# Other slots for eight early weight tiles, and the maxima of v two heads at a time, in a talking-heads attention with a gated MLP behind it

## The chip, the cores and the metric

One core of a Trainium2 chip runs the whole program. The metric is the device time of one execution in microseconds. Smaller is better. The median of three runs stands for a kernel, and one further execution was recorded by the hardware profiler.

## What is computed

```python
# attention: batch 4, heads 12, sequence 448, head_dim 64
scores = einsum('bhij,hg->bgij', q @ k^T / 8, w_pre)      # mixed over heads before the softmax
attn   = exp(scores - max) / (sum + 1e-9)                 # over the keys
attn   = einsum('bhij,hg->bgij', attn, w_post)            # mixed over heads behind it
x      = attn @ v, as 1792 tokens x 768
# gated MLP, w_gate and w_val 768 x 1536, w_out 1536 x 768; the MLP's weights come as 8-byte floats
out    = (1 / (1 + exp(-(x @ w_gate))) * (x @ w_val)) @ w_out
```

## The kernel before, in words

**Stages.** The program is one instruction stream per engine, written out by hand in program order. First comes the attention (`_attention`), up to about 344 us of the span. Behind it comes the MLP (`_Moe`), whose tasks a planner in the kernel has put in order. The MLP's first operands are prepared while the attention's last slots run.

**Blocks, units, slots.** A batch's 448 query rows are cut into four blocks of 120, 120, 120 and 88 rows, sixteen blocks in all. A block is cut into sets of ten rows, and two sets are a unit: six units in a block of 120, five in the last block of a batch, whose fifth unit holds one set. That makes 23 units a batch and 92 in all. The attention's main loop (L396) runs over slots s. The blocks begin at slots 0, 6, 12, 18, then 23, 29, 35, 41, then 46, 52, 58, 64, then 69, 75, 81, 87. A batch's last block is slots 18 to 22, 41 to 45, 64 to 68 and 87 to 91.

**What one slot issues.** GpSimd scales the sums of unit s+1 (`norm`, L228, result ss), VectorE takes their reciprocal (L229), and GpSimd scales the exponentials to fp16 (`scale`, L235, result ph, two instructions). TensorE mixes the heads of unit s+2 (`premix`, L211). VectorE takes row maxima (`rowmax`, L216, result nm). TensorE computes the scores of a pair of heads of a later block (`scores`, L157), and ScalarE and VectorE copy one half each out of PSUM (`keep`, L163). ScalarE takes the exponentials of unit s+2 (`expo`, L223, result e, with an accumulator read for the sums). VectorE computes the rest of the fp16 split (`p_lo`, L241, result pl, which reads e and ph from SBUF). Then come the small VectorE jobs of the plan (`v_max`, L175; `v_bound`), TensorE's second mix of unit s (`postmix`, L253), ScalarE's copy of it (`mix`, L261), and last the "tail": the product with v for an earlier block (`av`, L280) and the early weight steps. A second pair of scores in the same slot follows the tail.

**Which scores and products a slot has.** The scores of a block are issued five slots ahead of the block before it, so those of a batch's last block (88 rows, padded to 90) lie in slots 7 to 12, 30 to 35, 53 to 58 and 76 to 81. They take four matmuls where others take eight. Slots 13, 36 and 59 hold two pairs of scores. The products with v of a last block (88 columns) lie in slots 23 to 28, 46 to 51 and 69 to 74, and slots 18, 41, 64 and 87 hold two products.

**Early weight tiles.** Eight of the MLP's weight tiles (k = 0 to 7) are loaded and turned from 8-byte floats into fp32 within the attention. `EARLY_AT[k]` is a tile's base slot, and `early(k, step)` is issued at base + 1, 2, 3, 4 (four loads on SP's queue, L1028), + 6 and 7 (the first GpSimd step, in two halves, L1067, from int8 into the buffer `half`), + 8 (a GpSimd cast within `half`, L1075), + 9 and 10 (the last GpSimd step, in two halves, L1067), + 10 and 11 (two halves of `convert` on VectorE, L1083), + 11 and 12 (two ScalarE passes `sum_of`, L989, which take a sum into an accumulator and write their unwanted output into the first half of `half`), and + 13 (`keep_w`, a DMA that GpSimd issues, L1087). There is one buffer `half` for all tiles, and three raw buffers, used in turn. Tiles 3 and 7 also carry the steps of a bound (`early_bound`), from base + 13 on.

The tail of a slot is issued in the order in which the plan was filled, so a step of tile k stands ahead of one of tile k+1:

```python
    for k in range(moe.EARLY):
        for step, slot in enumerate((1, 2, 3, 4, 6, 7, 8, 9, 10, 10, 11, 11, 12, 13)):
            at(EARLY_AT[k] + slot, moe.early, k, step)
```

**Maxima of v.** `v_max(b, h)` reduces head h of v (256 elements a partition) to one number, 48 instructions in all. `v_bound(b, step)` makes a bound of them for each pair of batches; its step 0 is three small VectorE instructions.

Of the kernel before, what the change touches and what calls it, by code (L numbers as in the profile page):

```python
# [25 lines left out]
QUAD = 4  # L26
# [15 lines left out]
def _attention(ctx, tc, ins, B, H, S, D, xs, raws, make_moe):  # L42

    nc = tc.nc
# [47 lines left out]
    vm = const.tile([128, B * H], F32, name="vm")  # L92
# [73 lines left out]
    vt = {}  # L166
# [5 lines left out]


    def v_max(b, h):
        nc.vector.tensor_reduce(vm[:, H * b + h:H * b + h + 1], vt[b, h // QUAD][:, h % QUAD].rearrange("p j d -> p (j d)"),  # L175
                                axis=AX.X, op=ALU.max, apply_absolute_value=True)

    def v_bound(b, step):
# [116 lines left out]

    LEAD = 5
    SOFT = 2
    EARLY_AT = (5, 12, 19, 27, 34, 42, 49, 57)
    BOUND = (0, 6, 10, 11, 12, 13, 14)
    plan = {}  # L300

    def at(slot, fn, *args):
        plan.setdefault(slot, []).append((fn, args))

    def spread(i, n, s0, s1):
        return s0 + i * (s1 - s0) // n

    taken = {EARLY_AT[k] + slot for k in range(moe.EARLY) for slot in (10, 11)}
    for b in range(B):
        f = first[PB * b]  # L310
        for u in range(NQ):
            at(f + 2 + 2 * u, v_load, b, u)
        s = f + 5
        for h in range(H):
            s = max(s + 1, f + 6 + 2 * (h // QUAD))
            while s in taken:
                s += 1
            at(s, v_max, b, h)
        if b % 2:
            at(s + 1, v_bound, b, 0)  # L320
        if b == 1:
            for step, slot in enumerate(BOUND[1:]):
                at(s + 1 + slot, v_bound, b, step + 1)
        for c in range(NP if b else 0):
            at(spread(c, NP, first[PB * (b - 1)] + 6, first[PB * b - 1] - LEAD - 2), k_load, b, c)
# [15 lines left out]
# [3 lines that stand above are left out]
        if k % 4 == 3:  # L344
            for step, slot in enumerate((13, 14, 17, 19, 20, 21, 22, 22)):
                at(EARLY_AT[k] + slot, moe.early_bound, ("w", k // 4), step)

# [852 lines left out]
@with_exitstack  # L1200
def kernel(ctx, tc, B, H, S, D, ins, out):
    nc = tc.nc
    top = ctx.enter_context(tc.tile_pool(name="top", bufs=1))
    dram = ctx.enter_context(tc.tile_pool(name="dram", bufs=1, space=DRAM))
    xs = dram.tile([B, H * D // 128, 128, S], F32, name="xs")
    with tc.manual_schedule():
        raws = top.tile([128, 13 * H * D // 2], F32, name="raws")
        with ExitStack() as c2:
            moe = _attention(c2, tc, ins, B, H, S, D, xs, raws,
                             lambda NG: _Moe(tc, xs, ins, out, raws, NG, top))  # L1210
        moe.run()
# [72 lines left out]
```

## Time and profile before

| | us |
|---|---|
| median of 3 runs | 788.52 (788.35 to 790.19) |
| the profiled execution | 788.24 |
| its span, first to last instruction | 786.5 |
| TensorE busy | 760.4 (97%) |
| VectorE busy | 649.4 (83%) |
| ScalarE busy | 548.3 (70%) |
| GpSimd busy | 293.7 (37%) |

The granted TensorE clock is 0.998 of full speed over the span. Matmuls are pipelined and their ends are modelled, so a busy TensorE is not TensorE at its peak. What a slot takes is read from the start of one unit's premix (L211) to the start of the next unit's: slot s begins with the premix of unit s+2. The chain of waits, followed back from the last instruction of a stretch, names what released each piece.

### The profile page before, as it was taken

To read this page: it belongs to the slowest core of one execution; us is meant where nothing else is said; L and a number is where in the kernel's file an instruction comes from. 1 tells how busy PE (TensorE), PEld (TensorE's weight loads), DVE (VectorE), ACT (ScalarE), POOL (GpSimd) and SP (SyncE) were. 2 spreads that over 40 slices of the span, in tenths; PEclk is the share of its full clock that TensorE was granted. 3 is DMA by queue.
4 is the path that set the end of the run, shared out by engine and by line. 5 is a ranking of instruction groups with operands and counts; after the bars stand their busy time and mean duration, and the time that the engine had idled before them with its cause. 6 is when DMAs were issued, how large, how long until landed. Compare 5 with 4: busy or idle time off the path is not lost.

```text
span 786.5 us, 23288 instructions
## 1 busy us (share of the span) xinstructions
PE 760.4 (97%) x9530; PEld 417.6 (53%) x9530; DVE 649.4 (83%) x1116; ACT 548.3 (70%) x1058; POOL 293.7 (37%) x462
## 2 busy tenths in 40 slices
PE   7899999999999999888999999999999999999998
PEld 2455655565556555564555455555555555555554
DVE  4999999999989999999996989589876999997111
ACT  3887889788978888796875876577756784563000
POOL 1447776876786544410222222224222221010000
PEclk9999999999999999999999999999999999999999
DMA  5786568756875575839406284663567788995001
GB/s 183 232 255 223 192 231 260 252 193 227 284 261 186 183 226 186 250 105 321 143 27 224 92 301 152 251 222 141 198 205 263 277 313 312 383 346 206 36 36 70
DMA packets 80714, 166.13 MB, mean 211 GB/s; under 512 B 20448, under 2 KB 57664, under 8 KB 80608
## 3 DMA queue, kind: packets, MB, share of 16 engines
q1 hardware_dynamic: 72304, 132.88, 51.0%
q0 software_dynamic: 7728, 31.27, 10.3%
q8 instruction: 74, 1.21, 0.7%
q10 hardware_dynamic: 576, 0.51, 0.2%
q14 instruction: 32, 0.26, 0.1%
HBM read 87.77 MB, written 38.15 MB: 160 GB/s over the span
## 4 chain that ended last, share of the span: by engine, by line
PE 77%; ACT 9%; DVE 7%; DMA 3%; POOL 2%; issue 2%; SPq 0%; ACTq 0%; DVEq 0%; POOLq 0%
PE bank L1138 31%; PE bank L1149 18%; PE av L280 8%; PE pm L211 7%; PE qk L157 7%; PE mx L253 6%; ACT e L223 3%; ACT mix L261 2%; DVE nm L216 2%; DVE m L1122 2%; DMA k<-in_kp_dram 1%; ACT st L163 1%; ACT m L1117 1%; DVE m L1131 1%; DVE pl L241 1%
## 5 line engine op out<-in xcount | busy, mean ns | idle before, releaser
L1138 PEld LDWEIGHTS <-m 128*128 128x128 f16 x1512 | 147.5, 98 | 143.6 <-DVE m L1122 4.1
L1138 PE MATMUL bank<-m,m 128*128 128x448 f16 x1116 | 214.7, 352 | 4.6 <-DVE m L1122 3.2
L223 ACT ACTIVATE e<-pm,nm 128x448 f32<-128x448 f32 x180 | 115.2, 640 | 50.1 <-DVE nm L216 42.1
L235 POOL TENSOR_SCALAR ph<-e,ss 128x448 f16<-128x448 f32 x180 | 113.2, 641 | 55.3 <-DVE ss L229 31.3
L241 DVE SCALAR_TENSOR_TENSOR pl<-e,ss,ph 128x448 f16<-128x448 f32 x180 | 123.6, 725 | 1.2 <-POOL ph L235 1.2
L1149 PEld LDWEIGHTS <-m 128*128 128x128 f16 x756 | 74.0, 98 | 69.0
L216 DVE TENSOR_REDUCE nm<-pm 128x1 f32<-128x448 f32 x180 | 103.0, 613 | 7.2 <-PE pm L211 5.4
L253 PEld LDWEIGHTS <-ph 64*128 64x128 f16 x2880 | 67.6, 93 | 68.0 <-issue 34.5
L261 ACT ACTIVATE mix<-mx 128x960 f32<-128x960 f32 (+1 forms) x92 | 103.0, 1119 | 0.0
L157 PE MATMUL qk<-k,q 64*64 64x448 f32 (+2 forms) x640 | 94.9, 545 | 4.4 <-ACT st L163 2.8
L211 PE MATMUL pm<-T,w 64*64 64x448 f32 (+1 forms) x720 | 95.3, 560 | 1.3 <-ACT e L223 0.7
L280 PE MATMUL av<-mix,v 128*64 128x120 f32 (+1 forms) x1504 | 92.6, 267 | 1.4 <-ACT xt L290 1.4
L1149 PE MATMUL bank<-m,m 128*128 128x448 f16 x468 | 92.9, 352 | 0.0
L1075 POOL CAST raws<-raws 128x768 f16<-128x768 bf16 x36 | 40.6, 1127 | 117.4 <-ACT raws L1069 117.4
L253 PE MATMUL mx<-w2hi,ph 64*128 64x60 f16 x1440 | 70.9, 188 | 9.3 <-ACT mix L261 8.9
L1138 PE MATMUL bank<-m 128*128 128x448 f16 x396 | 77.9, 353 | 0.0
L280 PEld LDWEIGHTS av<-mix,v 128*64 128x64 f32 x1504 | 73.5, 137 | 6.2 <-ACT xt L290 1.7
L253 PE MATMUL mx<-w2hi,pl 64*128 64x60 f16 x1440 | 70.4, 187 | 0.2 <-DVE pl L241 0.2
L253 PE MATMUL mx<-w2lo,ph 64*128 64x60 f16 x1440 | 70.5, 187 | 0.0
L1165 DVE TENSOR_TENSOR m<-bank,m 128x448 f32<-128x448 f32 x72 | 44.4, 619 | 22.1 <-PE bank L1138 13.9
L253 PEld LDWEIGHTS <-pl 64*128 64x128 f16 x1440 | 61.7, 93 | 0.3 <-DVE pl L241 0.3
L228 POOL TENSOR_SCALAR ss<-ss 128x2 f32<-128x2 f32 (+1 forms) x92 | 30.2, 328 | 81.4 <-ACT e L223 79.0
(124 smaller groups left out, 1079.3 us busy)
## 6 DMA issues: line engine op xcount, KB each, us to landing
T<-st SPq DMA_DIRECT2D x176, 210.0 KB
m<-w SPq DMA_DIRECT2D x60, 384.0 KB
raws<-in_w_dram SPq DMA_DIRECT2D x28, 767.6 KB
hs<-m POOLq DMA_DIRECT2D x48, 224.0 KB, 3.2
m<-hs SPq DMA_DIRECT2D x15, 672.0 KB
w<-m POOLq DMA_DIRECT2D x21, 384.0 KB, 4.7
w<-raws POOLq DMA_DIRECT2D x20, 384.0 KB, 4.5
v<-in_vb_dram SPq DMA_DIRECT2D x12, 512.0 KB
```

What stands on the lines that cost most here:

```text
L157: nc.tensor.matmul(sc[e][s0:s1, :S], lhsT=q[rows, c, s0:s1], rhs=k[rows, :], start=True, stop=True)
L211: nc.tensor.matmul(pm[bank][64 * x:64 * x + 64, :S], lhsT=w1[rows], rhs=T[rows, x], start=True, stop=True)
L216: nc.vector.tensor_reduce(nm[:, i:i + 1], pm[bank][:, :S], axis=AX.X, op=ALU.max, negate=True)
L223: nc.scalar.activation(out=e_t[u][:, i], in_=pm[units[u][2][i]][:, :S], func=AF.Exp, bias=nm_t[u][:, i:i + 1], scale=1.0, accum_out=ss_t[u ...
L235: nc.gpsimd.tensor_scalar(ph[:, i], e_t[u][:, i], ss_t[u][:, i:i + 1], 1.0, op0=ALU.mult, op1=ALU.mult)
L241: nc.vector.scalar_tensor_tensor(pl[:, i], e_t[u][:, i], ss_t[u][:, i:i + 1], p_t[u][0][:, i], op0=ALU.mult, op1=ALU.subtract)
L253: nc.tensor.matmul(mx[:, x, i, jb * HK:(jb + 1) * HK], lhsT=p[rows, i, JB[jb]:JB[jb] + 128], rhs=w[rows], start=(k == 0), stop=(k == 2))
L261: nc.scalar.activation(out=out.rearrange("p g (y r) -> p y g r", r=HALF), in_=mx_t.pop(u), func=AF.Copy, scale=1.0 / (P_UP * W_UP))
L280: nc.tensor.matmul(av_t[bi][64 * i:64 * i + 64, c % 4, :n], lhsT=vt[b, u][:, h + i, jb, :], rhs=mixes[bi % 2][:, jb, 2 * c + i, :n], start ...
L1138: self.nc.tensor.matmul(self.f32(bank), lhsT=w[a][:, k], rhs=x[b][:, k], start=self.START[i] and k == r == 0, stop=k == self.KH - 1 and r ...
L1149: self.nc.tensor.matmul(self.f32(bank), lhsT=w[a][:, k], rhs=b[bb], start=self.START[i] and j == k == r == 0, stop=j == OUT_TILES - 1 and ...
L1165: self.nc.vector.tensor_tensor(self.f32(out), self.f32(bank), self.f32(snap), op=ALU.add)
```

## The change

`EARLY_AT` gets other base slots, `v_max` takes two heads in one instruction (a 2 x 256 input, two results) every second slot, and `v_bound` of batch 1 keeps its slot by an explicit line.

```diff
     def v_max(b, h):
-        nc.vector.tensor_reduce(vm[:, H * b + h:H * b + h + 1], vt[b, h // QUAD][:, h % QUAD].rearrange("p j d -> p (j d)"),
+        at = h % QUAD
+        nc.vector.tensor_reduce(vm[:, H * b + h:H * b + h + 2], vt[b, h // QUAD][:, at:at + 2].rearrange("p h j d -> p h (j d)"),
                                 axis=AX.X, op=ALU.max, apply_absolute_value=True)
...
-    EARLY_AT = (5, 12, 19, 27, 34, 42, 49, 57)
+    EARLY_AT = (-1, 6, 13, 19, 30, 37, 53, 60)
...
-        s = f + 5
-        for h in range(H):
-            s = max(s + 1, f + 6 + 2 * (h // QUAD))
+        s = f + 4
+        for h in range(0, H, 2):
+            s = max(s + 2, f + 6 + 2 * (h // QUAD))
             while s in taken:
                 s += 1
             at(s, v_max, b, h)
+        if b == 1:
+            s = f + 23
         if b % 2:
             at(s + 1, v_bound, b, 0)
```

Worked out from the code, the slots of each tile's five GpSimd steps, and of its two ScalarE passes:

| tile | steps before | passes before | steps after | passes after |
|---|---|---|---|---|
| 0 | 11-15 | 16, 17 | 5-9 | 10, 11 |
| 1 | 18-22 | 23, 24 | 12-16 | 17, 18 |
| 2 | 25-29 | 30, 31 | 19-23 | 24, 25 |
| 3 | 33-37 | 38, 39 | 25-29 | 30, 31 |
| 4 | 40-44 | 45, 46 | 36-40 | 41, 42 |
| 5 | 48-52 | 53, 54 | 43-47 | 48, 49 |
| 6 | 55-59 | 60, 61 | 59-63 | 64, 65 |
| 7 | 63-67 | 68, 69 | 66-70 | 71, 72 |

The pairs of maxima stand in slots 6, 8, 11, 13, 15, 18; 31, 33, 35, 37, 39, 42; 52, 54, 56, 58, 60, 62; and 75, 77, 79, 81, 83, 85. `v_bound` of batch 1 begins in slot 47 in both kernels, that of batch 3 in slot 86 instead of 87.

## Rows read from the trace of the kernel before

**Rows 1.** Busy time by stretch: window, its length, then each engine, clock, DMA.

```profile
400.00:420.00 20.00, 20.00 (x108) 10.32 (x106) 18.79 (x24) 12.05 (x20) 3.67 (x7) 1.00 0.39 131
```

**Rows 2.** Chain of waits, slots 80 and 81 (90-wide scores): start, us, what.

```profile
303.03 0.91 PE pm L211 x8
...
306.49 0.91 PE pm L211 x8
```

**Rows 3.** Chain of waits, slots 70 to 75 (products 88 columns wide).

```profile
269.78 0.91 PE pm L211 x8
...
285.77 0.91 PE pm L211 x8
```

**Rows 4.** Chain of waits, starts of slots 16, 18 and 23.

```profile
77.47 0.91 PE pm L211 x8
78.39 0.75 PE qk L157 x8
...
84.28 0.91 PE pm L211 x8
...
101.77 0.91 PE pm L211 x8
```

**Rows 5.** Chain of waits, early slots: GpSimd's small step of two units.

```profile
33.03 0.33 POOL ss L228
...
36.05 0.33 POOL ss L228
```

**Rows 6.** VectorE's maxima of v, 27 to 330 us: xcount | busy us, mean ns | idle.

```profile
L175 DVE TENSOR_REDUCE vm<-v 128x1 f32<-128x256 f32 x48 | 19.6, 408 | 0.0
```

**Rows 7.** Timeline of GpSimd, slots 56 to 58: start, us, instruction, [idle before].

```profile
219.15 0.19 POOL L228 TENSOR_SCALAR ss<-ss 128x2 f32<-128x2 f32 x1
...
220.94 2.43 POOL L1067 TENSOR_SCALAR raws<-raws 128x384 int16<-128x384 int8 x1
223.46 0.19 POOL L228 TENSOR_SCALAR ss<-ss 128x2 f32<-128x2 f32 x1
...
227.39 0.19 POOL L228 TENSOR_SCALAR ss<-ss 128x2 f32<-128x2 f32 x1
...
231.69 0.19 POOL L228 TENSOR_SCALAR ss<-ss 128x2 f32<-128x2 f32 x1
```

**Rows 8.** Timeline of VectorE beside it, slot 56.

```profile
221.04 1.27 DVE L241 SCALAR_TENSOR_TENSOR pl<-e,ss,ph 128x448 f16<-128x448 f32 x2
```

**Rows 9.** Timeline of TensorE: starts of slots 34, 38, 48, 53, 56 and 61.

```profile
139.55 0.61 PE L211 MATMUL pm<-T,w 64*64 64x448 f32 x4
...
155.73 0.61 PE L211 MATMUL pm<-T,w 64*64 64x448 f32 x4
...
189.85 0.61 PE L211 MATMUL pm<-T,w 64*64 64x448 f32 x4
...
207.05 0.61 PE L211 MATMUL pm<-T,w 64*64 64x448 f32 x4
...
217.44 0.61 PE L211 MATMUL pm<-T,w 64*64 64x448 f32 x4
...
238.82 0.61 PE L211 MATMUL pm<-T,w 64*64 64x448 f32 x4
```

**Rows 10.** Timelines of ScalarE (slots 24, 25) and GpSimd (slots 25, 26).

```profile
109.88 0.52 ACT L989 ACTIVATE raws<-raws 128x384 f16<-128x384 f32 x1
...
112.02 1.18 ACT L261 ACTIVATE mix<-mx 128x960 f32<-128x960 f32 x1
...
111.66 1.55 POOL L1067 TENSOR_SCALAR raws<-raws 128x384 int16<-128x384 int8 x1
...
115.09 1.20 POOL L1067 TENSOR_SCALAR raws<-raws 128x384 int16<-128x384 int8 x1
```

**Rows 11.** Timeline of VectorE, slots 86 to 88.

```profile
326.51 1.15 DVE L1122 SCALAR_TENSOR_TENSOR m<-m,one_w 128x384 f16<-128x384 f32 x2 [0.91 <-ACT m L1117]
...
330.60 0.21 DVE L999 STREAM_TRANSPOSE junk<-one_x 128x32 f32<-128x32 f32 x1
```

## The prediction, made before the changed kernel was run

> **What bounds the kernel now.** I read the page's shares first, then the chain of waits stretch by stretch, then the timelines of GpSimd and VectorE where the chain left TensorE. Behind the attention TensorE is busy without a gap [rows 1], so what the attention ends earlier or later, the kernel does too, nearly one for one. The change lies wholly within the attention, so the question is what bounds a slot there.
>
> The page shows VectorE at 83% and nearly full in the attention, and one would take it for the bound. The chain says otherwise. In most slots it runs from premix to scores to second mix to product and back to premix, with TensorE alone. With 90-wide scores a slot takes 306.49 - 303.03 = 3.46 us [rows 2]; with 120-wide scores and 120-wide products (84.28 - 77.47) / 2 = 3.40 us [rows 4]; with 88-wide products (285.77 - 269.78) / 5 = 3.20 us [rows 3]. I call these the floors. A second pair of scores adds about 0.75 us [rows 4], so slots 13, 36 and 59 have a floor of about 4.15. Only in slots 1 to 6, which have no product yet, is a latency loop longer than TensorE's work: from GpSimd's sums through VectorE's reciprocal and maxima, ScalarE's two exponentials and back to GpSimd, 36.05 - 33.03 = 3.02 us [rows 5]. The same loop turns in every slot, so the others have a slack of 3.46 - 3.02 = 0.44, 0.38 and 0.18 us. What delays the loop by less costs nothing.
>
> What the early steps cost today is then the time of a stretch less its floors. Slots 34 to 37: 155.73 - 139.55 = 16.18, floors 2 x 3.46 + 4.15 + 3.40 = 14.47, so 1.7 us. Slots 56 to 60: 238.82 - 217.44 = 21.38, floors 3 x 3.46 + 4.15 + 3.40 = 17.93, so 3.4 us. Slots 48 to 52: 207.05 - 189.85 = 17.20, floors 4 x 3.20 + 3.40 = 16.20, so 1.0 us [rows 9]. But slots 18 to 22, which hold all five steps of tile 1, take 101.77 - 84.28 = 17.49 us of unbroken TensorE work in the chain [rows 4]. **The batch's last block itself, in slots 18 to 22, costs nothing with steps in it.** The dear place is where the *scores* of a last block are computed (slots 30 to 35, 53 to 58).
>
> Why there: with 90-wide scores a GpSimd step that takes 1.20 us elsewhere [rows 10] takes 2.43 [rows 7]. VectorE's pair of pl starts 0.10 us behind it and runs its undisturbed 1.27 us [rows 8], and 2.43 is one after the other. GpSimd then is the loop: from one ss to the next 4.31 us with such a step and 3.93 with the cast (223.46 - 219.15, 227.39 - 223.46), and 4.30 again [rows 7].
>
> Of this the Trainium skill, page "SBUF — State Buffer", section "SBUF: two separate sides", says that the port pair that GpSimd and VectorE share is an exclusive lock, held for a whole instruction by the one that starts first. The rows agree that it is one after the other, but not on who wins: the step began 0.10 us ahead and yet took 2.43. By the page's order the step would keep its 1.2 us and pl would wait about 1.1; that is a rival's price below.
>
> **The change part by part.**
>
> *Steps leave slots 33 to 35 and 55 to 58.* Tile 3 goes to 25 to 29 and tile 6 to 59 to 63. The 1.7 and 3.4 us go; the double slots 36 and 59 still hold a first step (tiles 4 and 6), for which I leave 0.1 us each. **-4.9 us** (bounds -5.1 and -3.9: slot 14, behind the double slot 13, loses time today too).
>
> *Tile 0 goes to slots 5 to 9.* Slots 7 to 9 have 90-wide scores. Its cast and its last two steps then meet pl as in slots 56 to 58: 3.93 + 2 x 4.31 - 3 x 3.46 = 2.2 us, less the slack that is there on entry, about 0.3. **+1.9 us** (0.3 if the steps keep 1.2 us, 2.2 at most). Its steps in slots 5 and 6 lengthen a loop of 3.02 by under 0.1 each, which I leave out.
>
> *A new wait.* Tile 3's base is only six slots behind tile 2's, all others are seven or more apart. So in slot 25 tile 2's second ScalarE pass (base + 12) and tile 3's first GpSimd step (base + 6) meet. Both write the first half of the one buffer `half`, the pass stands first, and the step must wait for it. ScalarE issues the pass behind mix of slot 25, which starts at 112.02 today; the pass of the slot before began at 109.88, right behind its own mix, and took 0.52 and an accumulator read [rows 10]. So the step could start near 113.6 where GpSimd is free near 111.0, and end at 114.8 instead of 112.3. Queued behind it on GpSimd are the sums and ph of the next units; VectorE's reciprocal, pl, and TensorE's second mix wait for those. Slot 25 has 0.18 us of slack. **+2.4 us** (from 0, if the pass comes early, to 2.7).
>
> *Tile 2 to 19 to 23, tile 1 to 12 to 16.* The first takes the place that costs nothing today. Tile 1's first step falls into slot 12 with 90-wide scores, behind the issue of a DMA, and the next into the double slot: **+0.4** (0 to 0.9). Tile 3 in 25 to 29 costs there what tile 2 does today, beyond the wait: 0.
>
> *Tile 7 to 66 to 70, tile 5 to 43 to 47.* Three steps of each fall into the last block, where today's cost nothing; two fall into slots of floor 3.20, and the ScalarE passes (0.5 us each, in the loop) follow in such slots too. Today five steps cost 1.0 there. For tile 7 this is new: **+0.7** (0 to 1.6). For tile 5 it replaces 1.0: **0** (-1.0 to +0.6).
>
> *Loads.* Tile 0's four loads go to slots 0 to 3, ahead of the regroup DMAs of later slots on SP. The loop there waits for no DMA in the chain; 0 (to +0.5). All raw buffers have been read long before they are loaded again. The DMA issue of `keep_w` stands ahead of another tile's step on GpSimd in five slots (12, 19, 26, 43, 66) where it was four, and lies in the terms of tiles 1 and 3.
>
> *Maxima by pairs.* A single takes 408 ns [rows 6]. The pair is bounded by one and by two singles, 0.41 to 0.82 us; I take 0.7, near the upper end, since it reads twice the elements. VectorE is not the bound in any slot that holds one, so **0** whatever it saves (-0.3 to +0.5: 0.3 us more at once, in one slot of two, where other delays have used up the slack).
>
> *v_bound of batch 3* moves its three instructions from slot 87 to 86. VectorE bounds the last slots; there they end at 330.81, and in slot 86 VectorE has an idle 0.91 us [rows 11]. **-0.3** (-0.7 to 0).
>
> The sum: -4.9 + 1.9 + 2.4 + 0.4 + 0.7 + 0 - 0.3 = **+0.2 us**. The profiled execution took 788.24, 1.7 around its span of 786.5, and the median is 788.52. Since the difference is what I predict, 788.52 + 0.2 = **788.7 us**.
>
> **The rivals.**
>
> *The wait bites less or not at all* (pass and step turn out not to conflict, or mix comes early): 788.7 - 2.4 = 786.3. For it: no row of before shows such a wait for more than the order of issue, since no two tiles are six apart. Against: the code has both writing the same bytes.
>
> *GpSimd keeps its 1.2 us in slots 7 to 9*: 788.7 - 1.6 = 787.1, and with the first rival too 784.7. For it: steps elsewhere do. Against: what made the difference in slots 56 to 58 was there in each of three slots in a row.
> By the skill's order (the earlier instruction keeps the port) pl would wait 1.1 us in each of the three slots, which overruns the slack of 0.44 by some 0.6: 788.7 + 3 x 0.6 - 1.9 = 788.6, so it changes little; of this rival's chance below, half is its.
>
> *Slower: the slots of floor 3.20 make up nothing.* Their slack is 0.18 us, and after the change the passes of tiles 2, 5 and 7 fall into them (24, 25, 48, 49, 71, 72). If each pass shows its full 0.5 us and each step 0.3, tiles 5 and 7 come out at their upper bounds (+1.5 over my sum), tile 1 too (+0.5), and the wait at 2.7: 788.7 + 2.3 = 791.0, and with 2.2 for tile 0 791.3. It decides from about 0.2 us of ScalarE time per slot. Against: slots 70 to 74 stay at 3.20 right behind tile 7's second pass in slot 69 [rows 3].
>
> *The change doesn't do what it says*: of the 13 steps that lie in last blocks today (slots 18 to 22, 41 to 44, 64 to 67), ten still do. That costs nothing, as shown; it is in every case.
>
> **How the numbers follow.** Forecast as summed, no change: 0.57. No wait: 0.13. No stretch in slots 7 to 9: 0.10. Both: 0.05. Slower rival: 0.15. About 0.3% (2.4 us) is what a measurement of this kernel can tell from no change, so faster is below 786.2 and slower above 790.9. Faster gets the 0.05, half of the first rival and a little of the others' tails: 0.17. Slower gets the slower rival and 0.02 of the forecast's tail: 0.17. No change: 0.66. The range, 785.6 to 791.3, leaves out the case of both gains and the far end of the costs.
>
> **What would show each step.** Slots 30 to 35 and 53 to 58 at 3.46 us each, and no 2.4 us step there: the relief. Steps of 2.4 us and a cast of 2.1 in slots 7 to 9: tile 0's cost. GpSimd idle for some 2.5 us ahead of an L1067 in slot 25, released by ScalarE's L989: the wait. Slots 18 to 22 at 17.49 us as before. If VectorE, not TensorE, is in the chain of plain slots after the change, the prediction is wrong from the start; if the end of the attention moves and the end of the kernel does not follow, it is wrong in its carry-over.

## The result, and the profile after

| | before | after |
|---|---|---|
| median, us | 788.43 (787.95 to 790.19) | 794.07 (793.74 to 794.43) |
| the profiled execution, us | 788.24 | 794.43 |
| its span, us | 786.5 | 792.6 |
| TensorE busy, us | 760.4 | 763.0 |

The ratio is 1.0066, with a 95% interval from 1.0053 to 1.008: the change costs 5.6 us by the medians, 5.2 by the ratio. The forecast was 788.7 with a range of 785.6 to 791.3, and the kernel came out dearer than that range.

Behind the attention TensorE is as full as before [rows 1]. Busy time by stretch: window, its length, each engine, clock, DMA share, GB/s. The second line is a stretch that will matter.

```profile
410.00:430.00 20.00, 20.00 (x108) 10.36 (x106) 16.84 (x23) 11.35 (x21) 4.19 (x7) 1.00 0.50 169
134.00:150.00 16.00, 15.07 (x340) 9.58 (x332) 15.62 (x34) 14.81 (x35) 8.34 (x16) 1.00 0.88 280
```

So the loss lies in the attention, and first where the forecast saw the gain. Timeline of TensorE in the kernel after, at the starts of slots 34, 35, 38, 56 and 61, to be laid beside [rows 9]: start, us, instruction, idle before it and what ended that.

```profile
145.50 0.98 PE L212 MATMUL pm<-T,w 64*64 64x448 f32 x8
...
149.96 0.61 PE L212 MATMUL pm<-T,w 64*64 64x448 f32 x4 [0.93 <-issue]
...
161.58 0.61 PE L212 MATMUL pm<-T,w 64*64 64x448 f32 x4
...
224.03 1.77 PE L212 MATMUL pm<-T,w 64*64 64x448 f32 x8
...
245.06 0.61 PE L212 MATMUL pm<-T,w 64*64 64x448 f32 x4
```

Slots 34 to 37 took 16.18 us and now take 161.58 - 145.50 = 16.08. Slots 56 to 60 took 21.38 and now take 21.03. The GpSimd steps are gone from there, and 0.5 us came of it where I had booked 4.9. TensorE waits there for other things now. At 149.96 it stands still for 0.93 us, and no engine ended that wait. At 224.03 the eight matmuls of a premix take 1.77 us where they took 0.98 at 145.50: the second half waits for its copy T. The third thing is a store. Timeline of ScalarE of the kernel after, slot 58, and of TensorE beside it:

```profile
234.59 0.46 ACT L291 ACTIVATE xt<-av,sw 128x240 f32<-128x240 f32 x1 [1.70 <-DMA xs<-xt]
```

```profile
235.10 0.32 PE L281 MATMUL av<-mix,v 128*64 128x120 f32 x2 [0.79 <-ACT xt L291]
```

ScalarE may not write xt before the store of the block before has left it, and TensorE's product waits behind ScalarE.

The wait between tiles 2 and 3 is where the forecast put it. Timeline of GpSimd of the kernel after, slot 25, and of ScalarE beside it:

```profile
113.55 1.26 POOL L236 TENSOR_SCALAR ph<-e,ss 128x448 f16<-128x448 f32 x2 [0.37 <-PE qk L157]
117.36 1.20 POOL L1070 TENSOR_SCALAR raws<-raws 128x384 int16<-128x384 int8 x1 [2.55 <-ACT raws L992]
118.63 0.19 POOL L229 TENSOR_SCALAR ss<-ss 128x2 f32<-128x2 f32 x1
```

```profile
115.68 1.14 ACT L262 ACTIVATE mix<-mx 128x960 f32<-128x960 f32 x1
116.66 0.53 ACT L992 ACTIVATE raws<-raws 128x384 f16<-128x384 f32 x1
117.06 0.22 ACT L992 ACTIVATION_READ_ACCUMULATOR raws<-raws 128x1 f32 x1
```

GpSimd stands idle for 2.55 us until ScalarE's pass has ended, and the next units' sums queue behind the step. The stretched steps of tile 0 are there too (GpSimd of the kernel after, slots 7 to 9), and so are the pairs of maxima (VectorE, xcount | busy us, mean ns | idle):

```profile
47.83 2.07 POOL L1078 CAST raws<-raws 128x768 f16<-128x768 bf16 x1
...
51.77 2.44 POOL L1070 TENSOR_SCALAR raws<-raws 128x384 int32<-128x384 int16 x1
...
56.09 2.90 POOL L1070 TENSOR_SCALAR raws<-raws 128x384 int32<-128x384 int16 x1
```

```profile
L176 DVE TENSOR_REDUCE vm<-v 128x2 f32<-128x512 f32 x24 | 16.2, 675 | 0.0
```

But in slot 8 TensorE does not wait for these steps. It stops in the middle of sixteen matmuls of one product, at a matmul that waits for no semaphore (TensorE of the kernel after):

```profile
50.69 0.84 PE L281 MATMUL av<-mix,v 128*64 128x120 f32 x12
53.13 0.43 PE L281 MATMUL av<-mix,v 128*64 128x120 f32 x4 [1.60 <-issue]
```

**What such a stop is.** The trace also records DMA packets of 16,384 bytes in a queue that the profile's page calls "q8 instruction": 74 in the whole execution, beside 19,060 recorded matmuls and weight loads of TensorE, which is one packet for about 258 of them. In the stretch 50.50 to 53.20 of the kernel after, the DMA queues (packets, MB, share of 16 engines) were:

```profile
q1 hardware_dynamic: 375, 0.59, 70.0%
q8 instruction: 1, 0.02, 2.8%
```

I numbered TensorE's instructions (matmuls and weight loads in order of start) and set each stop without a releaser beside the packet before it:

| kernel | stop ahead of instruction | packet, us | TensorE goes on at | behind the packet |
|---|---|---|---|---|
| before | 5548 | 140.99 to 142.16 | 143.71 | 1.55 |
| after | 1460 | 50.63 to 51.85 | 53.13 | 1.28 |
| after | 5549 | 147.32 to 148.49 | 149.96 | 1.47 |
| e22 | 1204 | 45.52 to 46.68 | 48.27 | 1.59 |
| e22 | 1460 | 52.40 to 53.49 | 54.74 | 1.25 |
| e15 | 1460 | 49.53 to 50.74 | 52.28 | 1.54 |
| e17 | 4782 | 125.37 to 126.66 | 127.93 | 1.28 |

The stops lie at the same few places of the instruction stream in all of them: 1460 - 1204 = 256 instructions apart, or near a multiple of it where a few records are lost (4782 - 1460 = 3322, 13 x 256 = 3328), and TensorE goes on 1.25 to 1.6 us behind a packet's end. The same holds for all 37 waits of over 0.35 us that TensorE's matmuls show without a releaser in the attention of the 18 profiled kernels. Before and e1 do not stop ahead of instruction 1460, and there the packet had ended 2.66 and 1.93 us before TensorE came to it. I read the stops as TensorE out of instructions. The Trainium skill, page "Runtime: NRT & Kernel Launch", section "Instruction fetch mechanics", says that an engine streams its program through a queue of its own in blocks of 16 KiB, 256 instructions, at a cost that is mostly hidden. The rows agree on the block and on the distance; on the cost they differ, since stops of 0.6 to 1.6 us show at single boundaries in these kernels.

**Behind the stop the steps do reach TensorE.** Chain of waits of the kernel after, slots 8 to 11:

```profile
46.63 1.25 POOL ph L236 x2
47.88 2.02 POOL raws L1078
...
51.81 2.40 POOL raws L1070
...
56.12 2.87 POOL raws L1070
...
59.07 0.20 POOL ss L229
...
60.10 0.48 ACT e L224
```

The chain runs along GpSimd through all three stretched steps, and in slot 11, where VectorE's row maxima and ScalarE's exponentials come late behind the sums, TensorE loses 0.80 us. So in slot 8 TensorE loses 1.84 us at the stop, and with the steps, which come out last, 2.64 by slot 11. In slot 13 TensorE loses another 0.96: GpSimd's first step of tile 1 follows a DMA issue, the sums come late behind both, and a copy of ScalarE that TensorE waits for comes late behind the sums (GpSimd, VectorE and TensorE of the kernel after):

```profile
67.76 0.76 POOL L1090 DMA_DIRECT2D w<-raws  x1
68.56 1.67 POOL L1070 TENSOR_SCALAR raws<-raws 128x384 int16<-128x384 int8 x1
...
70.54 0.17 DVE L230 RECIPROCAL ss<-ss 128x2 f32<-128x2 f32 x1 [1.38 <-POOL ss L229]
...
72.52 0.98 PE L157 MATMUL qk<-k,q 64*64 64x448 f32 x8 [0.81 <-ACT st L163]
```

### The profile page after: what moved, and what is told of

The parts are those of the page before. It is cut to its first block, busy times and chain, and to the rows that moved or that the text cites. A ratio compares the mean times of both kernels' runs of the same rounds, so it can differ in the third digit from the quotient of the medians.

```text
span 792.6 us, 23264 instructions
## 1 busy us (share of the span) xinstructions
PE 763.0 (96%) x9530; PEld 418.6 (53%) x9530; DVE 649.1 (82%) x1092; ACT 548.8 (69%) x1058; POOL 293.4 (37%) x462
## 3 DMA queue, kind: packets, MB, share of 16 engines
q8 instruction: 74, 1.21, 0.7%
## 4 chain that ended last, share of the span: by engine, by line
PE 77%; ACT 9%; DVE 6%; DMA 3%; POOL 3%; issue 1%; SPq 0%; ACTq 0%; DVEq 0%; POOLq 0%
PE bank L1141 34%; PE bank L1152 18%; PE av L281 7%; PE pm L212 6%; PE qk L157 6%; PE mx L254 5%; ACT e L224 4%; DVE nm L217 2%; ACT mix L262 2%; ACT st L163 1%; DVE m L1125 1%; DMA xs<-xt 1%; POOL raws L1070 1%; ACT m L1120 1%; DVE pl L242 1%
## 5 line engine op out<-in xcount | busy, mean ns | idle before, releaser
L212 PE MATMUL pm<-T,w 64*64 64x448 f32 (+1 forms) x720 | 97.9, 560 | 2.7 <-ACT e L224 1.7
L229 POOL TENSOR_SCALAR ss<-ss 128x2 f32<-128x2 f32 (+1 forms) x92 | 33.1, 360 | 84.5 <-ACT e L224 82.3
L1168 DVE TENSOR_TENSOR m<-bank,m 128x448 f32<-128x448 f32 x72 | 44.6, 621 | 22.7 <-PE bank L1141 14.4
```

The source lines that it names most:

```text
L212: nc.tensor.matmul(pm[bank][64 * x:64 * x + 64, :S], lhsT=w1[rows], rhs=T[rows, x], start=True, stop=True)
L1168: self.nc.vector.tensor_tensor(self.f32(out), self.f32(bank), self.f32(snap), op=ALU.add)
```

## How the losses are counted

A slot's loss is its time, from premix to premix, less its floor from the prediction; a double slot's floor is read as 4.20 here, which is what such slots take in kernels that lose nothing there. Sums over slots of one profiled execution, in us and good to about 0.1, beside the measured ratio to before:

| kernel | ratio [95%] | 7-9 | 10-14 | 25-29 | 30-37 | 47-52 | 53-60 | 71-75 |
|---|---|---|---|---|---|---|---|---|
| before | 1 | 0.0 | 0.8 | 1.4 | 1.7 | 1.1 | 3.4 | 0.0 |
| after | 1.0066 [1.0053, 1.008] | 1.8 | 2.6 | 3.9 | 1.6 | 1.7 | 3.0 | 1.1 |
| e1 pairs alone | 0.9998 [0.998, 1.0015] | 0.0 | 1.3 | 1.6 | 2.3 | 0.7 | 3.8 | 0.0 |
| e3 after, no wait | 1.0028 [1.0013, 1.0044] | 2.9 | 1.2 | 1.5 | 1.6 | 1.5 | 2.5 | 1.0 |
| e4 no steps | 0.9977 [0.9965, 0.999] | 2.0 | 0.8 | 1.7 | 1.3 | 1.0 | 2.3 | 0.0 |
| e12 k spread | 1.0011 [0.9994, 1.0028] | 2.0 | 0.8 | 1.4 | 1.5 | 1.0 | 3.4 | 0.0 |
| e11 no steps, k spread | 0.9971 [0.9953, 0.9988] | 2.2 | 0.8 | 1.4 | 1.0 | 1.1 | 2.4 | 0.0 |
| e17 and no loads | 0.9933 [0.9908, 0.9957] | 1.4 | 0.8 | 2.6 | 0.2 | 1.1 | 0.4 | 0.0 |
| e13 e3, k spread | 1.0011 [0.9992, 1.003] | 3.5 | 1.2 | 2.0 | 0.8 | 1.5 | 0.3 | 1.1 |
| e14 other places | 0.9965 [0.9947, 0.9983] | 1.2 | 0.3 | 2.2 | 0.2 | 2.8 | 1.5 | 0.6 |
| e15 and later k | 0.9946 [0.9927, 0.9966] | 1.4 | 0.2 | 1.4 | 0.2 | 2.2 | 0.8 | 0.6 |
| e21 e15, tile 0 early | 0.9996 [0.9978, 1.0014] | 2.5 | 0.2 | 1.8 | 0.2 | 2.2 | 2.4 | 0.6 |
| e22 e15, its loads early | 1.0002 [0.9984, 1.002] | 3.3 | 0.2 | 2.0 | 0.2 | 2.1 | 0.8 | 0.6 |

Single executions of one kernel differ by more than most terms here: 35 executions of before took 785.8 to 792.7 us. Before, e4, e11, e12, e17 and e19 are the same program up to slot 13, and they lose 0.0, 2.0, 2.2, 2.0, 1.4 and 1.5 us in slots 7 to 9, so the 0.0 of before is its lucky end and the 1.8 of after is not above the others. The ratios come from 6 to 12 executions each beside 25 to 35 of before, except after (4 and 4).

## The experiments

### Are the steps what the last blocks lose? e4 and e6

e4 is before without the steps and conversions of tiles 3 and 6, so that it leaves a part of the weights out:

```
 early(k, step):      # the four loads stay
+    if k in (3, 6):
+        raw = self.free["R"][(k - 1) % 3]    # the tile before, converted
+        if step < 11: return                 # no GpSimd step, no convert
```

> Kernel before with the five GpSimd steps and two conversions of tiles 3 and 6 left out; their loads stay, and the ScalarE passes and the copy out of these two tiles read tile 2's and tile 5's values (so a part of the weights is not computed). Theory A, on which my forecast rested: the 1.66 us that slots 34 to 37 lose over their TensorE floors and the 3.39 us of slots 57 to 60 are the GpSimd steps in and ahead of them; without the steps these slots stand at their floors and the kernel takes about 784 us (0.994 of before). Theory B: these slots wait for their own data, the copies of staged scores that come late on SP's queue behind the loads of k and of raw tiles; the steps are no part of it, slots 34 to 37 lose 1.3 to 1.7 us and 57 to 60 2.5 to 3.4 us as now, and the time is 787.5 to 788.5 us (0.999 to 1.000).

It took 0.9977 of before, 1.8 us less, which lies between A and B. Without any step slots 30 to 37 still lose 1.3 us and slots 53 to 60 2.3, but at other places: slot 56, where before loses nothing, loses 1.0. TensorE of e4 there, a premix of 0.98 us drawn out to 1.98:

```profile
219.28 0.59 PE L211 MATMUL pm<-T,w 64*64 64x448 f32 x2
...
219.71 1.55 PE L211 MATMUL pm<-T,w 64*64 64x448 f32 x6
```

e6 spreads the loads of k that share SP's queue with the copies (in fact to slots 1 to 9, 15 to 30 and 38 to 53):

```
-  at(spread(c, NP, first[PB*(b-1)] + 6, first[PB*b-1] - LEAD - 2), k_load, b, c)
+  at(spread(c, NP, first[PB*b-5] - LEAD + 2 if b > 1 else 1, first[PB*b-1] - LEAD - 2), k_load, b, c)
```

> Kernel before, with one thing changed: the six loads of k of the second, third and fourth batch are spread over slots 1 to 11, 15 to 34 and 38 to 57 or so, where before issues them in slots 6 to 11, 29 to 34 and 52 to 57. Theory A (GpSimd's steps make the loss in the last block of a batch): nothing in those slots changes, 787.5 to 788.8 us (ratio 0.999 to 1.001). Theory B (late copies behind a full SP queue): most of the 1.66 us of slots 34 to 37 and of the 3.39 us of slots 57 to 60 goes, and some of slots 11 to 14; 783.5 to 785.5 us (0.994 to 0.996).

Both failed: 1.0041 [1.0023, 1.0059]. Slots 57 to 60 lost 0.36, 0.86, 1.47 and 0.69 us, within a hundredth what they lose in before, so with steps there the steps do hold them. The second batch's loads, now among the first loads of v, went with a loss of 3.6 us in slots 8 and 9. This is no clear price of theirs: e12, which leaves that batch alone, loses the same 2.0 in slot 8, and the 1.6 of slot 9 fell while the trace granted half speed (1.2 GHz) from 54.64 to 58.05 us. From the two I formed theory C: two limits lie close together, and a slot waits for the later.

### Both limits: e12, e11, e17

```
e12  before, k_load of the third and fourth batch in slots 15 to 30 and 38 to 53
e11  e4 with that
e17  e11;  early(k, step):  + if step < 4 and k in (3, 6): return    # no raw loads either
```

> Kernel before with only the loads of k of the third and fourth batch spread over slots 15 to 31 and 38 to 54 (the second batch's stay, so that slots 7 to 14 are those of before). Theory C: GpSimd's steps alone hold slots 34 to 37 and 57 to 60, which lose 1.4 to 1.7 and 3.2 to 3.4 us as before: ratio 0.999 to 1.001. Theory B (late copies alone): slots 34 to 37 and 57 to 60 recover 4 us, ratio 0.994 to 0.996.

> The kernel of e4 (before without the GpSimd steps and conversions of tiles 3 and 6; part of the weights is not computed) in which the loads of k of the third and fourth batch are spread over slots 15 to 31 and 38 to 54, where before has them in 29 to 33 and 52 to 56; the second batch's stay. Theory C, formed on e4 and e6: in the last block of a batch two limits lie close together, GpSimd's steps and the late copies of staged scores, and a slot waits for the later of the two, so that taking away one uncovers the other (e4 lost 1.3 us in slots 33 to 37 and 2.3 us in 56 to 60 without steps). With both gone slots 33 to 37 and 56 to 60 lose under 0.8 us together, 2.8 us less than in e4: 783.5 to 785.5 us, ratio 0.993 to 0.996. Rival D: what e4 still lost belongs to neither (the stores of results, the bound of v): 0.9965 to 0.999 as e4.

> The kernel of e11 (before without GpSimd steps and conversions of tiles 3 and 6, loads of k spread) in which the raw loads of tiles 3 and 6 are left out too, 3 MB in slots 28 to 31 and 50 to 53. e11 still lost 1.0 us in slots 34 to 37 and 2.4 us in 53 to 60. Theory C (late copies, whatever loads stand ahead of them): both fall, to under 0.4 and under 0.8 us, 2 to 3 us less in all, ratio 0.993 to 0.9955. Rival D (neither steps nor the queue): as e11, 0.996 to 0.999.

e12 came out as C says: 1.0011, and 3.4 us in slots 53 to 60. e11 did not: 0.9971, no better than e4, the loss moved to slots 53 to 56 and stayed 2.4. The spread loads of k now stood ahead of the copies there. So C in its first form, with the loads of k for the cause, fell too. e17 takes the raw loads of the two tiles out as well (eight of 192 KB, so 1.6 MB, not the 3 MB of the expectation), and then the loss is gone: 0.2 and 0.4 us, and 0.9933, 5.3 us below before by the ratio (interval 3.4 to 7.3). These are starts of slots 34, 38, 56 and 61 in e17, and all that TensorE waited for in 130 to 246 us (us in total, times, longest):

```profile
142.15 0.61 PE L211 MATMUL pm<-T,w 64*64 64x448 f32 x4
...
156.87 0.61 PE L211 MATMUL pm<-T,w 64*64 64x448 f32 x4
...
218.79 0.61 PE L211 MATMUL pm<-T,w 64*64 64x448 f32 x4
...
236.98 0.98 PE L211 MATMUL pm<-T,w 64*64 64x448 f32 x8
```

```profile
PE mx L253 <- ACT mix L261: 0.5, 2, 0.2
```

14.72 and 18.19 us, against floors of 14.52 and 17.98. So about the 4.9 us are there to be had, but in these kernels only where steps and loads go together.

### The wait: e3 and e13

```
-  self.sum_of(..., self.at[names[1]].bitcast(F16))
+  self.sum_of(..., None if k == 2 else self.at[names[1]].bitcast(F16))   # None: self.junk
```

> Kernel after, with one thing changed: the two ScalarE passes of tile 2 (slots 24 and 25) write the output that nobody reads into a scratch tile that is free in these slots, no longer into the half tile that tile 3's first GpSimd step of slot 25 writes, so that step waits for no ScalarE pass. If the wait makes the 3.3 us that slots 27 and 28 of the kernel after lose over their floors: they lose under 0.8 us, and the time is 2.5 to 3.3 us below the kernel after, 790.8 to 791.6 us (1.003 to 1.004 of before). If the loss there is late copies on SP's queue (loads of v in slots 25, 27, 29) or the steps themselves, it stays: 793.5 to 794.5 us (1.0065 to 1.008).

1.0028, so 1.0066 - 1.0028 = 0.0038 or 3.0 us below after, with intervals of about 0.0015 on either side of each, and slots 25 to 29 fell from 3.9 to 1.5. The wait is confirmed in place and size. In slot 59 of e3 TensorE shows the late copy by name:

```profile
232.79 0.59 PE L212 MATMUL pm<-T,w 64*64 64x448 f32 x2 [0.63 <-DMA T<-st]
```

e13 is e3 with the loads of k spread as in e12.

> The kernel of e3 (after, tile 2's ScalarE passes write their unread output elsewhere) with the loads of k of the third and fourth batch spread over slots 15 to 31 and 38 to 54. Theory C: with no step in slots 33 to 37 and 55 to 59 the late copies are the only limit there, so the 1.6 us of slots 34 to 37 and the 2.4 us of slots 58 to 60 that e3 lost go, all but some 0.8 us: ratio 0.998 to 0.9995, 786.5 to 788 us beside 788.4 of before. Rival D: it stays where e3 is, 1.002 to 1.004.

1.0011: a little short of the expected 0.998 to 0.9995, but slots 30 to 37 went from 1.6 to 0.8 and 53 to 60 from 2.5 to 0.3. With no step left there, spreading the loads of k does give the slots back in the profile, 3.1 us of them; the time fell by 1.3 us, less than its noise.

### Tile 0 in slots 5 to 9: e9, e16, e18, e21, e22

```
e9   before, EARLY_AT = (-1, 12, 19, 27, 34, 42, 49, 57)
e16  e12, and the second batch's k_load in slots 7 to 13 instead of 6 to 10
e18  e16, EARLY_AT as in e9
e21  e15 (below), EARLY_AT = (-1, 13, 19, 31, 37, 42, 54, 61)
e22  e15, at(EARLY_AT[0] + slot - 8, ...) for tile 0's four loads alone: slots 0 to 3
```

> Kernel before, with one thing changed: tile 0 alone goes to base -1 (its loads to slots 0 to 3, its GpSimd steps to slots 5 to 9), all other tiles stay. If the stretched GpSimd casts in slots 7 to 9 cost what the kernel after shows there (1.84 us in slot 8 and 0.80 in slot 11 over the floors): 1.9 to 2.6 us more, 790.3 to 791.0 us (1.0024 to 1.0033). If that loss belongs to the loads of tile 1, which the kernel after has in slots 7 to 10 and this one in slots 13 to 16: slots 8 and 11 stand at their floors and the time is 788.0 to 788.8 us (1.000).

1.0012 [0.9995, 1.0028], which settles nothing: 0.9 us by the ratio, and slot 8 loses 1.7 us in it, but 2.0 in e12 and 1.2 in e4, which have no step there. So I went on:

> The kernel of e12 (before; loads of k of the third and fourth batch in slots 15 to 30 and 38 to 53) in which the second batch's loads of k go from slots 6 to 10 to slots 7 to 13, nearer to their use in slots 13 to 17. Every kernel profiled since e4 loses 1.2 to 3.6 us in slots 7 to 9, with tile 0's steps there or not; the profiled execution of before lost nothing there. If that loss is late copies behind a full queue (theory C), slots 7 to 9 stand at their floors or lose under 0.7 us and the time is 1 to 2 us below e12: ratio 0.997 to 0.9995. If it has another cause, slot 8 loses 1 to 2 us as in e12, ratio 1.000 to 1.002.

> The kernel of e16 with tile 0 alone at base -1 (steps in slots 5 to 9, loads in slots 0 to 3). With the queue lighter in slots 6 to 10, what slots 7 to 11 lose beside e16 is tile 0's GpSimd steps alone. My forecast's step (the casts of slots 7 to 9 are drawn out and TensorE waits): 1.4 to 2.6 us more than e16 in slots 7 to 11, less 0.6 us that slot 14 gets back: 0.8 to 2.0 us above e16. If the kernel after lost its 1.84 us of slot 8 to late copies: under 0.4 us in slots 7 to 11, time -0.6 to 0 us beside e16.

e16 came to 1.0001 and 1.65 us in slots 7 to 9: moving k there did not free them. e18 was 1.0025, 1.9 us above e16, at the upper end of what I expected of the stretched steps; only its stops, of 1.4 and 2.3 us, were ahead of instructions 1204 and 1460, and no GpSimd step ended them. Its last two steps of tile 0 took 1.21 and 1.20 us and were not stretched at all. After the second the clock fell: the trace grants half speed (1.2 GHz) for 3.41 us from 56.96, and the stretch reads 0.85:

```profile
50.00:60.00 10.00, 7.67 (x132) 3.84 (x128) 5.16 (x12) 4.76 (x11) 5.67 (x9) 0.85 0.76 218
```

Hence the pair that parts steps from loads:

> The kernel of e15 with tile 0 alone moved from base 7 to the kernel after's base -1 (loads in slots 0 to 3, GpSimd steps in slots 5 to 9). If the drawn-out casts of slots 7 to 9 cost what I forecast and e18 against e16 showed: 1.5 to 2.5 us above e15, ratio 0.9965 to 0.998. If slots 7 to 9 lose only what late copies and late instructions cost there anyway: as e15, 0.994 to 0.9955.

> The kernel of e15 with the four loads of tile 0 alone moved to slots 0 to 3; its steps stay in slots 13 to 17. It tells the loads' share from the steps' share in what e21 loses. If the steps make the loss: as e15, 0.994 to 0.9955. If loads in the slots of the first loads of v make it, by pushing these and the copies back: 1 to 2.5 us above e15, 0.996 to 0.998.

e21 is 0.9996 and e22 1.0002 where e15 is 0.9946. With the loads alone in slots 0 to 3 the whole price is there (1.0002 - 0.9946 = 0.0056, 4.4 us; the intervals leave some 2 to 7); steps in slots 5 to 9 add nothing to it that these runs could tell, which is to about 2 us. TensorE of e22 and, last, of e15:

```profile
48.28 0.20 PE L254 MATMUL mx<-w2lo,ph 64*128 64x60 f16 x2 [1.42 <-issue]
...
54.74 0.32 PE L281 MATMUL av<-mix,v 128*64 128x120 f32 x2 [1.51 <-issue]
```

```profile
52.28 0.32 PE L281 MATMUL av<-mix,v 128*64 128x120 f32 x2 [1.17 <-issue]
```

The packet ahead of instruction 1460 ended at 53.49 in e22 and at 50.74 in e15, but e22 had already lost 0.4 and 1.4 us in stops before it. In the seven kernels with tile 0's loads in slots 0 to 3, TensorE stops for over 0.35 us ahead of instruction 1204 in six, for 0.6 to 1.6 us; in the eleven others it does in two (e4 and e11, 0.65 and 0.58). The profiled execution of e22 is 2.9 us behind that of e15 at slot 88, and 1.9 of these come in slots 7 to 9; the rest of the 4.4 was not traced.

### Does any added load do this? e19

```
+  for slot in range(14, 19):
+      for step in (0, 1) if slot % 2 else (2, 3):
+          at(slot, moe.early, 2, step)
```

> Kernel before with one suspected cost added: ten reads of 192 KB from HBM, two in each of slots 14 to 18 (the first pieces of tile 2, into its own still unused buffer; the same bytes come again in slots 20 to 23). No engine's work changes. Before loses 0.79 us in slot 14 and nothing in 15 to 24 but the constant 0.38 us of slot 20. Theory C (a busy set of DMA engines brings copies, stores and TensorE's instructions late): TensorE stops in slots 16 to 22 where no semaphore or only a DMA ends the wait, 1 to 4 us in all, ratio 1.001 to 1.005. If DMA load is harmless there: under 0.3 us in these slots, ratio 0.999 to 1.001.

1.000 [0.9987, 1.0013]: not here. Slots 15 to 24 lost what they lose in before, the 0.38 us of slot 20. Before and e19 in slots 15 to 18:

```profile
72.00:86.00 14.00, 14.00 (x332) 8.26 (x330) 13.54 (x29) 12.74 (x29) 8.90 (x16) 1.00 0.52 165
```

```profile
72.00:86.00 14.00, 13.70 (x324) 8.12 (x320) 13.66 (x30) 11.73 (x29) 8.36 (x13) 1.00 0.78 241
```

The added reads raise the DMA share from 0.52 to 0.78, and that is harmless here. In 134 to 150 us, where both kernels lose, before stands at 0.83 and after at 0.88; but before stands at 0.90 in 40 to 50 us and loses nothing, and e22 at 0.76 in 40 to 55 us, where it loses most. So the average share doesn't tell which loads cost time; the order in which transfers stand ahead of each other may, but no run here shows it.

### The pairs alone: e1

The kernel after with `EARLY_AT` as before, so that the changed `v_max`, its loop and `v_bound` stay.

> Kernel before with the other half of the change alone: the maxima of v two heads in one instruction, tiles at their old places, the first step of batch 1's bound in slot 47 as before. My forecast's term for it is 0 (and -0.3 us where batch 3's bound leaves slot 87): 787.8 to 788.8 us, ratio 0.999 to 1.001. If instructions of 675 ns in VectorE's order cost more than two of 408 ns apart, as they stand ahead of the row maxima: 0.5 to 1.5 us more, 1.0005 to 1.002.

0.9998 [0.998, 1.0015]. The pairs cost and bring nothing that shows, to about 1.5 us.

### A version that beats both: e14 and e15

```
-  EARLY_AT = (-1, 6, 13, 19, 30, 37, 53, 60)
+  EARLY_AT = (7, 13, 19, 31, 37, 42, 54, 61)          # steps in 13 to 29, 37 to 52, 60 on
-  (..., 10, 10, 11, 11, 12, 13)
+  (..., 10, 10, 11, 12, 13, 13)                       # ScalarE's passes one slot later
-  self.sum_of(..., self.at[names[1]].bitcast(F16))
+  self.sum_of(..., raw[:, self.WE:].bitcast(F16))     # into the tile's own dead half
   # k_load as in e12; e15 also as in e16
```

The tiles' bounds follow one slot later.

> The kernel after with other places: tiles at bases 7, 13, 19, 31, 37, 42, 54, 61, so that no GpSimd step of a tile stands in slots 7 to 12, 30 to 36 or 53 to 59; every ScalarE pass writes its unread output into the dead second half of its own tile and one slot later, so that no step waits for a pass; the loads of k of the third and fourth batch spread over slots 15 to 31 and 38 to 54. Theory C: beside e13 the loss of slots 7 to 13 through tile 0's steps (2 to 3 us) goes too; three tiles between slots 13 and 29 and two between 37 and 52 cost some 0.5 to 1 us more in slots of floor 3.20; ratio 0.994 to 0.998, 783.8 to 786.8 us. If the raw loads of tiles 3 and 6, in slots 32 to 35 and 55 to 58, make the copies late just as the loads of k did: 0.998 to 1.001.

> The kernel of e14 with the second batch's loads of k in slots 7 to 13 instead of 6 to 10. e14 lost 1.15 us in slot 8. Theory C: that goes, 784.5 to 786.5 us, ratio 0.994 to 0.9965. Else as e14: 0.9955 to 0.9975.

e14 took 0.9965, e15 0.9946 [0.9927, 0.9966]: 784.73 us, 4.3 below before by the ratio. The late k of e15 did not give what I expected of it: slots 7 to 9 still lose 1.4 us. It is ahead of e14 in slots 53 to 60 and 47 to 52, within what single executions differ, and the intervals of the two ratios overlap.

## Why the prediction was wrong, point by point

**What bounds the kernel.** Right: TensorE, with the floors as read, and the attention's end moves the kernel's. The profiled spans differ by 6.1 us and the starts of slot 88 by 7.3; the stage behind takes 455.1 to 457.6 us in all kernels run, without order.

**Steps leave the last blocks, -4.9: the step that failed.** The forecast was +0.2 and the attention came out at +7.3; 4.4 of these 7.1 us are this term. I wrote that what the steps cost is the time of a stretch less its floors. That is what the stretch loses to everything. In slot 34 of before it was not a step at all (TensorE of before):

```profile
143.71 0.61 PE L211 MATMUL pm<-T,w 64*64 64x448 f32 x4 [0.63 <-issue]
```

That "issue" was there to be read, and none of my rivals had it. In slots 57 to 60 the steps did hold TensorE (e6, e12), but behind them stood late copies and late stores, and slots 53 to 60 still lose 2.3 us when the steps go (e4). Relief by the steps alone: 1.8 us in e4, 0.5 us in after's slots, against 5.3 in e17, where the loads go too. The change itself also brought the four loads of tile 4 from slots 35 to 38 to 31 to 34, and those of tile 6 from 50 to 53 to 54 to 57, beside the loads of k in 29 to 33 and 52 to 56, which the term did not look at. In e13 these tile loads stay and those of k are spread, and slots 30 to 37 and 53 to 60 lose 1.1 us instead of the 5.1 of before. In slots 57 to 60 the rows on which I rested the term were right about who was late last, and silent about who was late next.

**Tile 0, +1.9: the mechanism was there, but not alone.** Slots 7 to 14 lose 3.6 us more in the profiled execution of after than in that of before: 1.84 in slot 8, 0.80 in slot 11 and 0.96 in slot 13. The steps are drawn out as forecast, 2.07 to 2.90 us, and the chain through them is what ends last in slots 8 to 11, which lose 2.64. But TensorE's missing instructions took 1.84 of these in slot 8 already, and in e22 the loads cost no less without any step there; what the steps alone would cost no run shows, since their loads have to come ahead of them. Since the profile of before is a lucky one in slots 7 to 9, the nearness of 2.64 to 1.9 is in part luck. Moving tile 0 alone, steps and loads, cost 0.9 us on before (e9), 1.9 on e16 (e18) and 3.9 on e15 (e21). Nor does a start 0.10 us ahead of pl always draw a step out: in before the steps at 168.96, 193.23 and 196.50 us start that far ahead and keep 1.20 to 1.21 us, while the first instruction of pl takes 0.92 to 0.93 instead of 0.67. What decides between the two was not found.

**Loads, 0 (to +0.5): wrong.** I asked whether the loop waits for a DMA in the chain, and it did not. I did not ask what else the same DMA engines carry. The four loads in slots 0 to 3 cost 4.4 us in e22; e9 and e18, which move them together with the steps, cost 0.9 and 1.9.

**The new wait, +2.4: right.** 2.55 us of idle GpSimd, 2.5 us in slots 25 to 29, 3.0 us in e3.

**Tile 1, +0.4:** slots 10 to 14 rise by 0.45 in e3 and e13, right; by 1.8 in after, of which 0.80 in slot 11 belongs to tile 0's last step and 0.96 in slot 13 is tile 1's first step behind the DMA issue, as forecast and at the upper bound. **Tile 7, +0.7:** 1.06 in slots 72 to 74. **Tile 5, 0:** +0.65 in slots 47 to 52, the upper bound. So tiles 5 and 7 do show in slots of floor 3.20, as in the slower rival, though the rival put this at 2.3 us over the sum where it is about 1.0; how much of it is ScalarE's passes was not separated. **Pairs, 0:** right (675 ns, e1). **v_bound, -0.3:** not seen; slots 82 to 88 take 22.6 us in before and 22.7 in after.

With 0.5 for 4.9 and 3.6 for 1.9 + 0.4, the sum by profile is -0.5 + 3.6 + 2.5 + 1.1 + 0.65 = 7.3, as the start of slot 88 has it.

What stays open: in what order the DMA engines serve instruction packets among copies and loads, whether copies came late through those engines or through the order of the DMAs on SP's queue, and why slot 8 loses 0 in one execution and 2 us in another of the same program up to there.

## What to carry to other kernels

What a stretch loses over its floor is the later of several things; before booking it as the price of one, take that one out and see what is late next. Here the steps alone were worth 1.8 us of 4.9 (e4), and the rest came only together with the loads. A wait that the profile ends with "issue" is a finding, not a rest: look in the DMA queues of the same stretch, instructions included. A load costs what it delays, and that hangs on its place: four loads at the start of the loop cost 4.4 us in e22, ten added ones in slots 14 to 18 nothing in e19. So the place of the loads of a prefetched tile can matter as much as the place of its work.

## What the runs showed of the hardware

As I read the rows, TensorE's own instructions come in packets of 16,384 bytes over the DMA engines that carry the data, and at such a 256-instruction boundary it stood still for 0.4 to 1.8 us, in e18 for 2.3, with no semaphore involved, until 1.25 to 1.6 us behind the end of a packet. What made the packets late was not measured. Between kernels of one instruction order the places stay, and only the arrival of the packets moves. Stops of 2.3 us in e18 and 1.8 us in e6 were followed by 3.41 us at half clock, one of 1.8 us in e12 was not.
